# A fused linear-attention and mixer kernel: u of batch 1 is transposed by the DMA queue of SP, under a new hand-written order for all engines

## The chip, the cores and the metric

The kernel runs on one core of one Trainium2 chip. The metric is device time in microseconds (us) of one execution. Three runs of the kernel before gave 172.86, 173.35 and 173.45 us; the median, 173.35 us, is the time before.

## The reference, cut to what matters

Four batches (B = 4) are computed, each in two halves. First an attention with a decaying state, with 8 heads, 768 time steps and 48 values per head:

```python
f = 1.0 / (1.0 + np.exp(-f_logit))
for t in range(S):
    state = f[:, :, t, :, None] * state + np.einsum('bhd,bhe->bhde', k[:, :, t], v[:, :, t])
    y[:, :, t] = np.einsum('bhd,bhde->bhe', q[:, :, t], state)
```

Then, on x = y written as 768 tokens by 384 channels, a mixer over tokens and one over channels:

```python
h = np.maximum(xt @ w_tok1, 0.0) @ w_tok2        # xt is x transposed
u = x + h.transpose(0, 2, 1)
h2 = np.maximum(u @ w_ch1, 0.0) @ w_ch2
return u + h2
```

## The kernel before, in words

**Attention.** A batch's 768 steps are cut into 6 chunks of 128. For each chunk ACT forms the logarithm of f (`exp` and `ln`, L371 and L372; for batch 0, where two chunks are interleaved as a pair, L392 and L388), POOL or DVE splits it into a high and a low part (`lo`, L379, L401), PE sums it along time (`sums`, L461 and L462; batch 0 L615 and L618), ACT takes two exponentials of the sums (`G` and `Gi`, L471 and L473; batch 0 L628 and L630), DVE multiplies them onto q and k (`gated`), and q and k are transposed (`turn`: by PE at L500, or at L503 by a transfer that SP issues for all of batch 3; the copies of PE's result are `turned`, on DVE or on ACT). PE forms the scores (L413) and the chunk's own contribution to the state (`parts`, L429). The state goes from chunk to chunk: `tsum` on DVE, `state` (L577) on DVE or POOL, and two copies into a bf16 tile (`spread`, into `state_bd`, L277 on ACT or L281 on POOL), which the next chunk's `y` (L560 and L564; batch 0 `within` L719 and `y` L743) reads. `glast` (L481) is a small transfer of SP that brings the decay of a whole chunk to where the state needs it; it waits for `grow` on ACT (L477).

**Mixer.** Per batch: 12 products `tok1` (L757), the copies `h1T`, 6 pairs of products `tok2` (L773), the additions `u` (L789) on DVE, a bf16 copy `u_bf` on ACT or POOL, then u is transposed into `uT`, 24 groups `ch1` of three products (L826) that read `uT` and `w_ch1`, their copies `zT` (L357 on ACT, L359 on DVE), 18 groups `ch2` of four products (L845), 6 additions (L851) and 6 stores (L855). A `ch1` of half 0 needs the rows 0 to 2 of `uT`, one of half 1 the rows 3 to 5.

**The two ways to transpose u.** For a batch in `UTURN` SP issues two transfers, each of which transposes three tiles of `u_bf`; for another batch PE transposes tile by tile and ACT or DVE copies the result out of PSUM:

```python
        if b in UTURN:
            for th in range(2):
                tts = range(3 * th, 3 * th + 3)
                add(("ut", b, th), SP, lambda th=th: nc.sync.dma_start_transpose(...
        for tt in range(0 if b in UTURN else NCH):
            ...
            add(("ut", b, tt), PE, turn, need=["ident", ("u_bf", tt)], bank=pm, kind=mms(*[C] * 3))
            copies(("uT", b, tt), (DVE, ACT), lambda tt=tt: uT[:, tt, :, :].rearrange("p d t -> p (d t)"),
```

**The order.** Every step is recorded as an operation with a number, and nothing chooses at run time: `Plan.run` (L125 to L140) walks through the string `ORDER` (L36 to L80) and issues the operations in that order. A token is an operation's number; a letter behind it names the engine where there is a choice (A is ACT, D is DVE, G is POOL), and `:n` the PSUM bank that it takes. `w512`, `s11` and the like are products without use, which keep PE busy. So each engine executes its operations in the order of the string, each waits for what it reads, and an engine that waits holds up all that stands behind. The loads from HBM are issued by POOL, in the same queue as its arithmetic (L266, and L272 for weights); SP's queue holds `glast`, the transposes and the stores.

Of the kernel before, what the change touches and what calls it, by code (L numbers as in the profile page):

```python
# [37 lines left out]
38 50 53D 54 12D 39 52D 25D 55 100:0 15G 40 58 105:1 56D 57D 102 59 10G 137:2 104 41 11D 30D 107 114:3 60D 142:4 101 42  # L38
110 106 108 31A 103 62 119:1:0 139 18D 109 115 145 61D 111:5 143 112 125 144 180:6 141 138 147 113A 116D 43 151:2 146
126A 130 118:3:4 140 44 127A 117:5:1 123 182 152 175:0 153A 4G 122 45 121 176 131G 148:3 120 177 149 64 156:4:2 183 181  # L40
178 124:0:5 150A 162 63 184 186:6 179 187 185 132A 134 47 128D 154:3:4 188A 189:1 158 190 133G 191D 163G 66 157 165A
193:3:6 136A 169 155:1:4 135A 164G 197 67 192:2:5 159 46 160 336 195 w512 w128 161:4:6 170G 337 196 339 338G 173 198 340
166 194:2 172A 341G 199:5:1 129A 200 171A 68 174A 204 201D 358:0 342 167D 208:2 203A 209 202G 205D 215:3 359 65 206 210
361 211 207D 216 212 217 343 213 218 219 214D 360 220 344G 366:7 168D 221A 242 238 369 230:2 69 231 222:4 223 232 367
226:3 227 73 243 224 368 234 250:0 244A 228 235 239 245A 246:7 71 251D 247A 363 248:1 394:0 237A 249D 70 364:7 236A 233
256:1 240A 225 252:6 16G 272:2 345 241D 72 396 276:4 253D 348 254:5 257D 270:6 397 74 255D 229 274:1 398 395 371 48
296:5 346 362 278:0 275A 347D 370 304:3 351 273D 277A 372:1 365D 279A 280:2 349 297D 298:0 271A 373D 350G 402:4 290:6
305D 75 292:5 281D 291A 374:3 299D 293A 78 375:6 352 376:2 386 403 286:5 76 377 404 284:6 378 79 264:0 258:7 379 285D 77
381A 262:3 259D 265A 282:6 263A 81 399 382:7 283A 300:0 385 287A 400:3 387 380A 302:5 407 405 384D 391:2 406 408:4 80
401D 393A 431:1 301A 409D 260:6 353G 303A 388D 410:0 261A 412:5 383A 414 411:6 389G 392A 268:7 415 434 413 266:2 435  # L50
390A 423 294:0 269A 419:3 416G 267D 433 462:7 87 439:6 424 420A 422 469:2 470 441 463 417G 288:5 421A 418G 432 464 83
471 289D 428:3 295A 311:1 429D 82 316:0 425D 430A 436 90 440 317 426A 442 318 85 472 312 86 313 93 465 437:6 314 91
443:3 319 438A 321:1 320 444D 96 447:0 445:5 99 446:4 448 322 450 427G 331:6 449 97 306:0 457 590 84 587 458 454:5 323
588 451G 455D 584 332 452G 324 585 453G 326:4 92 466 459:1 589G 327 460A 586G 328 89 467 473 474 468A 610:3 475D 461A
307 593 329 479:2 611 476:4 612 480 482:1 456A 485:7 477 596 481G 488:2 483 478A 308 94 486 594 602:1 489 484G 491:7 604
615 496:4 88 498:2 605 494:5 333 499D 497D 606 595G 613 495D 616:2 492 512:5 490G 487A 309 646:7 603 354 334 500:0 524:3
647 617D 513A 508:6 607 501A 510:5 591 525D 502:0 493A 608:1 511D 592G 599 506:3 503D 609D 504:0 95 528:5 507A 505D 509A
638:4 529D 597 522:0 639 618:5 598G 523D 640 619:6 648 620:3 630 98 641 534:0 623 544:6 629 642 600 625G 520:4 624G 614
545A 621 355 530:2 649 631 514:1 622 521A 675:7 531A 651 516:3 515A 643 518:2 601D 356 536:1 519A 635:4 677 537D 526:2
517A 535A 644:1 676 626:3 645D 652:0 628A 550:5 627A 527D 559:6 653D 632G 551A 678 683:2 634G 633G 656:5 679 818 655:7  # L60
659 654:3 684 650 560 660G 685 658 830 661G 542:2 667 662A 538:3 636A 666 637A 561 680 824 672:4 821 686 554:0 833 657
539A 552:7 668 831 673D 663:3 540:5 562 681:1 541A 713:6 819 714 682D 687:5 664A 555 820G 553A 688D 674A 556 669G 665A
357 834 691:4 557 689:3 671A 690:7 543A 693 564:0 827 692 670A 715 836:3 822 694 706:2 698:1 702 695G 548:4 699D 835G
696A 707 708 701 825 565 697G 839 700D 823G 532:7 840 837 716 703:1 533D 838 709 549D 546:5 704D 717 569:4 705D 710 718
843:1 719D 711 570 846 547D 712D 574:6 847 845 826D 844 720:2 828 841 723:5 729:1 848 870:3 721 829G 849 726:7 871 575
727 722G 735:2 724 842 732:7 736 725A 566 730 728A 737G 877:2 872 733 738 576 880 734G 912:7 731A 832G 571 873 739 852:1
572 878 579:5 567 879 905:4 855 330 882 580 857A 881 577 856G 913 874 581 863 914 875 851:1:6 582 850:7:2 907 886:0 876
861 756:5 864D 742:3 862 865G 762:6 743A 853 760:1 906 889 908 867:3 854 764:2 883 866A 780:4 757A 765D 890G 768:7 761A
763D 892G 772:2 310 910 769A 583 858:6 891A 758:1 335 773A 746:7 868A 315 859A 740:2 568 747D 781A 909 766:5 898 860A
741D 325 919:4 759A 899G 885:0:7 767A 884:6:2 897 776:1 888 754:5 750:0 887 784:6 751A 896 744:2 869A 785D 893:7 777D  # L70
902:3 911 901G 778:6 755D 900G 782:1 745D 779A 915 770:5 903A 573 894A 941:6 916 942 752:2 771A 786:0 753D 943 934:5 922
787A 748:2 783D 923G 944 813:0 749D 924G 904D 925G 935 774:2 895D 936 937 775A 803:7 917:2:3 918:1:4 921 804 929 805 920
808:4 806 926:3 930 809 927A 931:1 945 814 932A 946 938 939 947D 793:7 940A 928D 933A 810 954:1 963:3 960:5 964 957:6
788:2 965A 958 948:3 811 959G 789 961 949 951:4 962G 798:5 952 950A 967 799 955 794 956G 953G 795 966 800 815 812 790
807 563 1008:1 1014:4 1002:3 1015D 998:6 801 1003A 1004:4 791 988:5 816 1005A 992:2 999D 990:4 796 968:6 989D 797 991A
1010:7 1009A 802 993A 972:4 558 792 974:1 973D 817 1000:2 1011D 578 984:4 1001A 982:7 975A 994:2 978:1 996:5 979D 980:0
985D 997A 970:1 983A 995D 986:4 969D 1041:2 1012:6 1006:7 976:5 1007D 1036:3 971D 977A 987A 1013D 1046:7 1042 981A 1043
1026:0 1044 1031:6 1047 1037 1048 1027 1021:2 1032 1033 1022 1034 1038 1035 1045 1028 1039 1023 1049 1029 1050 1016:7
1040 1024 1017 1025 1030 1018 1019 1020
# [68 lines left out]
def kernel(  # L148
# [603 lines left out]
    def mixer(b):  # L752
# [14 lines left out]
        for tt in range(NCH):  # L767
# [23 lines left out]
            if b == 0:  # L791
# [124 lines left out]
```

## Time and profile before

| | |
|---|---|
| median of three runs | 173.35 us |
| the profiled execution, its own time | 173.47 us |
| its span (first to last instruction) | 171.7 us |
| granted clock of PE, mean | 0.996 |
| PE busy | 162.2 us, 94% of the span |
| DVE, ACT, POOL busy | 123.3, 105.9, 90.8 us |
| first `sums` of batch 0 on PE | 7.23 us |
| first `sums` of batch 1 on PE | 26.30 us |
| first `ch1` of batches 0, 1, 2, 3 | 33.60, 72.80, 113.55, 144.55 us |
| last `ch2` of batch 3 ends | 168.15 us |

The span is shorter than the execution's own time by 1.77 us, which lies before the first and behind the last instruction. A row of the timeline gives start and length in us, engine, line, operation, the tile written and the tiles read, the count, and in brackets the idle time ahead of it with what ended it. PE's products overlap: one that lasts 0.33 us starts 0.16 us after the one before.

### The profile page before, as it was taken

Reading aid. Unit: us, or ns where it says so; the run is one execution under the profiler, and the core shown is the slowest. Engines: PE = TensorE matmul, PEld = TensorE weight load, DVE = VectorE, ACT = ScalarE, POOL = GpSimd, SP = SyncE. Lnnn points to the kernel's source line nnn. Section 1 sums busy time; section 2 is a strip of 40 time slices with the busy share of each in tenths; the row PEclk is TensorE's granted clock in tenths of the full one; section 3 lists DMA queues with packets and bytes.
Section 4 is the critical chain, followed back from the end, with each engine's and each line's share of the span. In section 5 each row is a group of like instructions: output and inputs, shape, how many; then the busy total and the mean of one; then the engine's idle time right before and its main releaser. Section 6 shows DMA issues by size and latency. Waiting matters only on the chain.

```text
span 171.7 us, 4436 instructions
## 1 busy us (share of the span) xinstructions
PE 162.2 (94%) x1753; PEld 103.2 (60%) x1753; DVE 123.3 (72%) x262; ACT 105.9 (62%) x240; POOL 90.8 (53%) x131
## 2 busy tenths in 40 slices
PE   6998688999999989999999999999999999999991
PEld 3476565666766645666757665565766656566660
DVE  5589986899995662999777889696976380754051
ACT  5999869995995615979898844959441420542000
POOL 8999678959959598897841933411220031000000
PEclk9999999999999999999999999999999999999998
DMA  5999999999999999969999190978370008250024
GB/s 143 226 171 223 202 196 189 185 144 171 185 196 188 148 139 52 56 83 214 106 143 79 8 130 7 189 166 239 111 168 4 0 7 242 96 211 0 0 96 181
DMA packets 89572, 22.72 MB, mean 132 GB/s; under 512 B 82288, under 2 KB 88736, under 8 KB 89552
## 3 DMA queue, kind: packets, MB, share of 16 engines
q0 software_dynamic: 69600, 13.77, 92.6%
q1 hardware_dynamic: 19952, 8.69, 19.1%
q8 instruction: 13, 0.21, 0.5%
q14 instruction: 7, 0.06, 0.1%
HBM read 25.17 MB, written 4.72 MB: 174 GB/s over the span
## 4 chain that ended last, share of the span: by engine, by line
PE 74%; POOL 11%; DMA 7%; ACT 3%; issue 2%; DVE 1%; POOLq 0%; DVEq 0%
PE ps L826 27%; PE ps L845 24%; DMA f_sb<-in_f_logit_dram 7%; PE ps L757 4%; PE ps L773 4%; POOL qk_sb L266 4%; PE ps L500 3%; PE ps L413 3%; POOL v_sb L266 2%; PE ps L564 2%; PE ps L429 2%; PE ps L461 2%; PE ps L462 2%; PE ps L560 1%; PE ps L811 1%
## 5 line engine op out<-in xcount | busy, mean ns | idle before, releaser
L826 PE MATMUL ps<-uT,w_ch 128*128 128x384 bf16 x288 | 52.6, 326 | 0.0
L845 PE MATMUL ps<-w_ch,zT 128*128 128x384 bf16 (+2 forms) x300 | 52.6, 320 | 0.0
L357 ACT ACTIVATE zT<-ps 128x384 bf16<-128x384 f32 x55 | 25.2, 491 | 21.5 <-PE ps L826 21.1
L845 PEld LDWEIGHTS <-zT 128*128 128x128 bf16 x300 | 27.7, 98 | 17.0
L826 PEld LDWEIGHTS <-w_ch 128*128 128x128 bf16 x288 | 26.8, 97 | 16.3
L359 DVE TENSOR_SCALAR zT<-ps 128x384 bf16<-128x384 f32 x41 | 21.4, 552 | 13.0 <-PE ps L826 12.6
L541 DVE TENSOR_TENSOR AmT<-ps,tri_bf 128x512 bf16<-128x512 f32 x36 | 23.4, 684 | 2.6 <-PE ps L413 2.4
L851 DVE TENSOR_TENSOR x_nat<-x_nat,ps 128x384 f32<-128x384 f32 (+2 forms) x25 | 12.8, 533 | 11.3 <-PE ps L845 11.1
L379 POOL TENSOR_TENSOR Llo<-L 128x384 bf16<-128x384 f32 x15 | 12.4, 834 | 11.8 <-ACT L L372 11.7
L266 POOL DMA_DIRECT2D qk_sb<-in_q_dram x16 | 15.7, 986 | 2.9 <-DMA f_sb<-in_f_logit_dram 2.3
L266 POOL DMA_DIRECT2D v_sb<-in_v_dram x16 | 15.8, 990 | 2.7 <-DMA f_sb<-in_f_logit_dram 1.7
L266 POOL DMA_DIRECT2D qk_sb<-in_k_dram x16 | 15.8, 990 | 0.0
L281 POOL CAST u_bf<-x_nat 128x384 bf16<-128x384 f32 x10 | 5.0, 508 | 14.6 <-issue 10.1
L277 ACT ACTIVATE x_bf<-ps 128x384 bf16<-128x384 f32 x15 | 7.0, 486 | 8.8 <-PE ps L564 8.8
L281 POOL CAST state_bd<-state 48x192 bf16<-48x192 f32 x22 | 8.0, 363 | 8.0 <-PE ps L560 3.0
L757 PE MATMUL ps<-x_bf,w_tok 128*128 128x384 bf16 x48 | 11.9, 326 | 0.0
L789 DVE TENSOR_TENSOR x_nat<-x_nat,ps 128x384 f32<-128x384 f32 x21 | 10.5, 546 | 1.6 <-PE ps L773 1.6
L490 DVE TENSOR_TENSOR qk<-qk_sb,GG 128x768 bf16<-128x768 bf16 x18 | 10.8, 615 | 0.0
L577 POOL TENSOR_TENSOR state<-tsum,glast 128x192 f32<-128x192 f32 x9 | 4.6, 507 | 10.4 <-PE ps L826 4.9
L471 ACT ACTIVATE GG<-ps 128x384 bf16<-128x384 f32 x18 | 8.9, 492 | 1.9 <-PE ps L462 1.0
L371 ACT ACTIVATE f_sb<-f_sb 128x384 f32<-128x384 f32 x18 | 9.1, 524 | 1.3 <-DMA f_sb<-in_f_logit_dram 1.2
L372 ACT ACTIVATE L<-f_sb 128x384 f32<-128x384 f32 x18 | 9.5, 526 | 0.2
(101 smaller groups left out, 264.3 us busy)
## 6 DMA issues: line engine op xcount, KB each, us to landing
out_dram<-x_nat SPq DMA_DIRECT2D x23, 192.0 KB, 2.4
f_sb<-in_f_logit_dram POOLq DMA_DIRECT2D x3, 1152.0 KB, 11.9
f_sb<-in_f_logit_dram SPq DMA_DIRECT2D x3, 384.0 KB, 4.0
qk_sb<-in_q_dram POOLq DMA_DIRECT2D x12, 96.0 KB, 7.7
qk_sb<-in_k_dram POOLq DMA_DIRECT2D x12, 96.0 KB, 7.2
w_ch<-in_moe_w_ch_dram POOLq DMA_DIRECT2D x2, 576.0 KB, 12.8
v_sb<-in_v_dram POOLq DMA_DIRECT2D x12, 96.0 KB, 7.5
w_ch<-in_moe_w_ch_dram POOLq DMA_DIRECT2D x1, 1152.0 KB, 10.4
```

Source lines behind the costliest of these rows:

```text
L266: lambda eng=eng, into=into, of=of: eng.dma_start(out=into, in_=of),
L281: nc.gpsimd.tensor_copy(out_, in_)
L357: nc.scalar.activation(out_, in_, AF.Relu, bias=0.0, scale=1.0)
L359: nc.vector.tensor_scalar(out_, in_, 0.0, None, ALU.max)
L379: op.fn = lambda: (nc.vector if op.engine == DVE else nc.gpsimd).tensor_tensor(lo, full, hi, ALU.subtract)
L490: add(("gated", b, c, *names), DVE, lambda n=n: nc.vector.tensor_tensor(qk[it][:, n, :, 0:D], qk_sb[nb][:, n, :, c, :], GG[i][:, n], ALU.m ...
L541: add(("masked", b, c, p), DVE, lambda half=half, made=made: nc.vector.tensor_tensor(half, made(), tb4, ALU.mult), need=["tri_bf"], make=[ ...
L757: add(("tok1", b, rt, kt), PE, lambda rt=rt, kt=kt, pm=pm: nc.tensor.matmul(banks[pm.at][:, 0:DM], lhsT=w_tok1[:, kt, rt * 128:(rt + 1) * ...
L789: nc.vector.tensor_tensor(to, un, banks[pm.at][:, 0:DM], ALU.add)
L826: nc.tensor.matmul(banks[pm.at][:, 0:384].rearrange("p (n t) -> p n t", t=128), lhsT=w[:, kt, c0:c0 + 128], rhs=uT[:, rows3, kt, :], start ...
L845: nc.tensor.matmul(banks[pm.at][:, 0:n1 - n0], lhsT=zT[:, kt, tt * 128:(tt + 1) * 128], rhs=w_ch2[:, kt, n0:n1], start=(kt == 0), stop=(kt ...
L851: add(("sum", b, tt, n0), DVE, lambda un=un, pm=pm, n=n1 - n0: nc.vector.tensor_tensor(un, un, banks[pm.at][:, 0:n], ALU.add), make=[("x_n ...
```

## The change

`UTURN` gains batch 1, so that its u is transposed by two transfers of SP. The 6 transposes of PE (18 products) and the 6 copies of batch 1 go, two transfers come, the program has 1041 operations in place of 1051, and the numbers behind them move down by 10. The whole string `ORDER` is new: order, engines and banks of all operations. (The file is one line shorter: L826 of before is L825 after.)

```diff
-UTURN = (2, 3)
+UTURN = (1, 2, 3)
 ...
 ORDER = """
-w512 w512 w512 s11 32 0G 6G 33 8G 20D 9D 5G 34 13D 7G 1 21G 35 2 24A 23A 27D 3A 37 26A 29D 14D 28 49 17D 36 19D 51 22G
...
+w512 w512 w512 s5 32 5G 33 21G 20D 18G 7D 34 0D 14D 1 6G 2 24A 23D 8D 22G 35 26D 27D 11G 15D 36 19D 49 10D 25D 9D 37 29D
...
```

Among the products without use, `s11` becomes `s5`, and the pair `w512 w128` that stood behind the scores of batch 0 becomes one `w128` further ahead.

**ACT in the first 25 us.** Before, these rows (tiles of batch 0 until `f_sb_76`, which is f of batch 1; `zT` holds the turned q or k, `state_bd` is `spread`):

```order
L277 ACTIVATE zT<-ps_118 128x1024
L277 ACTIVATE state_bd_97<-state 48x4x48
L277 ACTIVATE x_nat_99<-ps_117 128x384
L277 ACTIVATE x_bf_102<-ps_117 128x384
L371 ACTIVATE f_sb_76<-f_sb_76 128x8x48
L372 ACTIVATE L_78<-f_sb_76 128x8x48
L371 ACTIVATE f_sb_76<-f_sb_76 128x8x48
```

After, the same place, up to the first logarithm of batch 1:

```order
L627 ACTIVATE GG_81<-ps_117 128x384
L632 ACTIVATE gpair_120<-ps_117 128x8
L276 ACTIVATE zT<-ps_112 128x1024
L276 ACTIVATE zT<-ps_115 128x1024
L276 ACTIVATE state_bd_98<-state 48x4x48 x2
L276 ACTIVATE zT<-ps_112 128x1024
L370 ACTIVATE f_sb_76<-f_sb_76 128x8x48 x2
L371 ACTIVATE L_78<-f_sb_76 128x8x48
```

Three of the four turned tiles of ACT now stand together right ahead of batch 1's f, and two `exp` stand ahead of the first `ln`. Further ahead, the `ln` of chunks 4 and 5 now stands before that of chunks 2 and 3, behind both `exp`. On PE the first `sums` of batch 1 moves up: it now stands ahead of `parts` of chunk 4, `within` of chunks 2 and 4, and `y` of chunks 2, 3 and 4 of batch 0, behind two `tok1`.

**POOL towards the end of batch 1's attention.** Before (`qk_sb_71` and `v_sb_74` are loads of batch 2, `glast_90` is the decay of chunk 4 of batch 1):

```order
L266 DMA v_sb_74<-in_v_dram 128x8x48 x2
L281 CAST state_bd_98<-state 48x4x48
L266 DMA qk_sb_71<-in_k_dram 128x8x48
L266 DMA v_sb_74<-in_v_dram 128x8x48
L577 TENSOR_TENSOR state<-tsum,glast_90 128x192
L281 CAST state_bd_97<-state 48x4x48 x2
```

After (`f_sb_76` is f of batch 3, a whole batch; `x_nat_100` is u of batch 1):

```order
L265 DMA qk_sb_71<-in_q_dram 128x8x48
L280 CAST state_bd_97<-state 48x4x48
L265 DMA qk_sb_71<-in_q_dram 128x8x48
L576 TENSOR_TENSOR state<-tsum,glast_90 128x192
L265 DMA qk_sb_71<-in_k_dram 128x8x48 x2
L265 DMA qk_sb_71<-in_q_dram 128x8x48
L265 DMA f_sb_76<-in_f_logit_dram 128x48x48
L378 TENSOR_TENSOR Llo<-L_77 128x8x48 x3
L265 DMA v_sb_74<-in_v_dram 128x8x48 x3
L265 DMA qk_sb_71<-in_k_dram 128x8x48
L280 CAST u_bf<-x_nat_100 128x384
```

Before, 13 loads stand between f of batch 2 and that `state`; after, 4 do. The load of f of batch 3, which stood behind three `u_bf` copies, now stands ahead of the `lo` steps of batch 2 and of both copies of u that POOL makes for batch 1.

**SP, from the last `glast` of batch 1.** Before, only `glast` and one store stand here:

```order
L481 DMA glast_89<-grow_94 128x1x4
L481 DMA glast_90<-grow_92 128x1x4
L855 DMA out_dram<-x_nat_99 128x384
L481 DMA glast_88<-grow_93 128x1x4
L481 DMA glast_90<-grow_92 128x1x4
L481 DMA glast_89<-grow_94 128x1x4
```

After:

```order
L480 DMA glast_88<-grow_93 128x1x4
L801 DMA_TRANSPOSE uT<-u_bf 128x9x128
L480 DMA glast_89<-grow_94 128x1x4
L480 DMA glast_88<-grow_93 128x1x4
L480 DMA glast_90<-grow_92 128x1x4
L801 DMA_TRANSPOSE uT<-u_bf 128x9x128
```

The first transpose, of tiles 0 to 2, stands behind the last `glast` of batch 1; between it and the second, of tiles 3 to 5, stand the `glast` of chunks 1, 0 and 2 of batch 2. All stores now stand behind the transposes of batch 1.

More of the change, by code (lines that the diff above doesn't have):

```diff
@@ L42 @@
[L42 to L61, printed above, removed]
@@ L77 @@
[L77 to L79 removed]
+w512 w512 w512 s5 32 5G 33 21G 20D 18G 7D 34 0D 14D 1 6G 2 24A 23D 8D 22G 35 26D 27D 11G 15D 36 19D 49 10D 25D 9D 37 29D
+50 12D 4D 51 40 3A 53D 54 28 52G 58 39 13D 105:0 59 38 55 100:1 61D 42 60D 108 106 56D 102 175:2 41 107 57D 101 104
@@ new lines @@
+956 953:2 949G 798:4 954 799 796 548 955G 779 957 800 780 801 785 806 802 797 960:0 786 563 974:4 792 978:7 975D 962:6
+979A 992:4 994:7 993A 976:2 963A 958:4 977D 964:6 781 959A 982:2 995D 782 980:5 787 986:7 807 981A 1000:4 987D 1002:5
+1004:7 1003A 998:1 961A 1005D 972:5 990:7 984:0 991A 966:3 985A 970:7 967A 996:0 965A 971D 983A 988:3 999D 1006:7 973D
+989D 1016:1 1001D 1036:3 968:5 1031:4 969D 1011:2 997D 1026:5 1032 1017 1018 1012 1021:0 1033 1013 1022 1014 1037 1034
+1023 1019 1035 1027 1015 1024 1020 1038 1028 1039 1040 1007 1029 1025 1008 1030 1009 1010
```

54 lines of the change are left out of this document (35 added, 19 removed).

## The prediction

> **What bounds the kernel now.** I read the table of stages first (busy time of each engine in stretches of the span), then PE's waits, then the timeline at those waits. In the table the first column is the length of the stretch, then busy time and count of each engine, granted clock, DMA share and GB/s.
>
> ```profile
> span 171.7 us, 4436 instructions
> 7.00:26.00 19.00, 16.30 (x418) 12.10 (x415) 16.49 (x39) 16.64 (x37) 16.42 (x23) 1.00 1.64 195
> 34.00:60.00 26.00, 26.00 (x294) 17.16 (x293) 22.08 (x46) 20.01 (x47) 20.53 (x25) 1.00 2.00 172
> 60.00:68.00 8.00, 6.92 (x62) 4.25 (x60) 3.58 (x7) 2.15 (x6) 7.76 (x12) 1.00 1.76 105
> 79.00:114.00 35.00, 34.93 (x374) 22.07 (x371) 29.38 (x59) 27.07 (x63) 17.67 (x23) 1.00 1.36 110
> 114.00:145.00 31.00, 31.00 (x278) 19.35 (x276) 20.17 (x40) 12.49 (x29) 5.55 (x13) 1.00 0.40 102
> ```
>
> From 34 us on PE is full, 26.00 of 26.00 and 31.00 of 31.00, except in 60 to 68, where it lacks 1.08 of 8.00 while POOL is full. So PE's own work, and the waits before 34 us and at 60 to 68, set the end; a product less is time less, and a wait elsewhere that reaches PE is time more. Behind PE's last product lies a tail (sum, store, end) that the change leaves as it is: the last `ch2` in the new list is again row 0 of batch 3. The profiled execution took 173.47 us for a span of 171.7; it is 0.12 above the median of 173.35. I add terms to 173.47 and take 0.12 off at the end.
>
> **Term 1: PE's transposes of batch 1, -1.0.** This row is one of the chain that ended last:
>
> ```profile
> 71.10 0.50 PE ps L811 x9
> L811 PE MATMUL ps<-ident,u_bf 128*128 128x128 bf16 x36 | 3.5, 219 | 0.1
> L279 DVE COPY uT<-ps 128x384 bf16<-128x384 bf16 x10 | 3.3, 349 | 0.0
> ```
>
> Nine products advance the chain by 0.50, so the 18 of batch 1 take 1.0, in stretches where PE is full. The six copies that go (0.35 each on DVE) free engines on which PE does not wait there; I take nothing for them.
>
> **Term 2: PE's waits at 61.8 and 64.9, -1.1.** PE's own list of waits, and the timeline:
>
> ```profile
> PE ps L560 <- POOL state_bd L281: 1.1, 2, 0.7
> 61.83 0.33 PE L560 MATMUL ps<-state_bd,qkT 128*128 128x96 bf16 x4 [0.68 <-POOL state_bd L281]
> 64.87 0.33 PE L560 MATMUL ps<-state_bd,qkT 128*128 128x96 bf16 x4 [0.39 <-POOL state_bd L281]
> 43.68 2.27 POOL L266 DMA_DIRECT2D f_sb<-in_f_logit_dram  x1
> 57.91 0.88 POOL L266 DMA_DIRECT2D v_sb<-in_v_dram  x1 [1.74 <-DMA f_sb<-in_f_logit_dram]
> 61.38 0.40 POOL L281 CAST state_bd<-state 48x192 bf16<-48x192 f32 x1
> 63.52 0.50 POOL L577 TENSOR_TENSOR state<-tsum,glast 128x192 f32<-128x192 f32 x1
> ```
>
> Both `y` wait for a copy of the state by POOL, which had stood 1.74 us at a load: seven loads are issued behind f of batch 2, and the next begins only when that f has landed. Everything behind it on POOL is 1.74 late, more than the 0.68 that PE lacks. After, 4 loads stand between that f and this `state` where 13 stood, and POOL reaches it before its `tsum` is there. What waits instead is the load of f of batch 3, the eighth behind f of batch 2; behind it stand three `lo`, the first of which PE reads some 3 us later by my count, and the u copies of term 4. If POOL is late all the same, this term is 0.
>
> **Term 3: the beginning, +1.1.** Rows of before:
>
> ```profile
> 7.64 0.85 ACT L392 ACTIVATE f_sb<-f_sb 128x768 f32<-128x768 f32 x1
> L388 ACT ACTIVATE L<-f_sb 128x768 f32<-128x768 f32 x2 | 1.7, 840 | 0.0
> 11.94 0.51 ACT L630 ACTIVATE GG<-ps 128x384 bf16<-128x384 f32 x1
> 12.31 0.52 ACT L628 ACTIVATE GG<-ps 128x384 bf16<-128x384 f32 x1
> 18.67 1.02 ACT L277 ACTIVATE zT<-ps 128x1024 bf16<-128x1024 bf16 x1 [0.20 <-PE ps L743]
> 22.18 0.53 ACT L371 ACTIVATE f_sb<-f_sb 128x384 f32<-128x384 f32 x1 [1.20 <-DMA f_sb<-in_f_logit_dram]
> L281 POOL CAST state_bd<-state 48x192 bf16<-48x192 f32 x22 | 8.0, 363 | 8.0 <-PE ps L560 3.0 <-DVE state L577 2.8 <-DVE state L549 1.5
> L379 POOL TENSOR_TENSOR Llo<-L 128x384 bf16<-128x384 f32 x15 | 12.4, 834 | 11.8 <-ACT L L372 11.7
> 22.87 0.89 PE L719 MATMUL ps<-v_sb,zT 64*128 64x48 bf16 x32
> 24.60 0.74 PE L719 MATMUL ps<-v_sb,zT 64*128 64x48 bf16 x32
> 26.13 0.33 PE L743 MATMUL ps<-state_bd,zT 128*128 128x96 bf16 x4 [0.79 <-ACT state_bd L277]
> 26.30 0.34 PE L461 MATMUL ps<-L,tri_bf 128*128 128x384 bf16 x1
> 27.67 0.33 PE L743 MATMUL ps<-state_bd,zT 128*128 128x96 bf16 x4 [0.38 <-POOL state_bd L281]
> 29.63 1.79 PE L773 MATMUL ps<-h1T,w_tok 128*128 128x384 bf16 x10
> ```
>
> Before, ACT had no work left at 21 us and stood until f of batch 1 had landed (22.18). After, ACT has more ahead of that f. From the `exp` at 7.64, which begins when the last f of batch 0 has landed: one `exp` and two `ln` at 0.84 (2.5), 12 `G` and `Gi` at 0.37 from start to start (4.4), four turned tiles at 1.02 (4.1), four `spread` at 0.36 (1.4; POOL's take the same), small ones 0.9, together 13.3. Waits inside: 0.75 for `sums` of chunk 3 (its `ln` now stands last, then two more `lo` on DVE), and about 0.8 for the transposes of chunks 0 to 3. So f of batch 1 is begun at 22.7; `exp`, `exp`, `ln` at 0.53 end at 24.2, `lo` on POOL (0.83) at 25.1, and PE begins `sums` of batch 1 there, 1.2 sooner than at 26.30. But of the work that lay before it, from 22.87 to 26.30 less the wait of 0.79, 2.4 us now lie behind, and two `tok1` (0.3) lie ahead: 2.1. PE is 2.1 - 1.2 = 0.9 behind. The waits that follow in before (0.38 at a `y` of batch 0, some 0.4 until 34 us) I set against those that I find in the new list: second `sums` of batch 1 behind a further `lo`, 0.4, `y` of chunk 5 0.3, scores of batch 1 and `tok2` behind DVE's queue of masks, 0.3: +0.2 net. Sum +1.1. Bounds: if ACT's waits vanish, the landing of f binds and `sums` begins at 24.6, +0.6 instead of +1.1, and without the waits behind it 0; if DVE's queue is 1.5 later still, +2.6.
>
> **Term 4: the wait for the two transfers, +0.3.** No transfer of this kind ran beside loads in before: the ten that there are lie at 105.9 us and later. The rows nearest are those of `glast` (2 KB) in three windows, and of a store among loads; last column, issue to landing:
>
> ```profile
> uT<-u_bf SPq DMA_TRANSPOSE x4, 2.9
> glast<-grow SPq DMA_DIRECT2D x2, 2.0 KB, 7.6
> glast<-grow SPq DMA_DIRECT2D x5, 2.0 KB, 5.0
> glast<-grow SPq DMA_DIRECT2D x5, 2.0 KB, 2.0
> out_dram<-x_nat SPq DMA_DIRECT2D x1, 192.0 KB, 4.2
> out_dram<-x_nat SPq DMA_DIRECT2D x23, 192.0 KB, 2.4
> 71.60 0.65 PE ps L845 x4
> 70.78 0.33 PE ps L773 x2
> 44.78 0.45 PE ps L500 x8
> L789 DVE TENSOR_TENSOR x_nat<-x_nat,ps 128x384 f32<-128x384 f32 x21 | 10.5, 546 | 1.6 <-PE ps L773 1.6
> ```
>
> The windows are 40 to 60 us (f of batch 2 in flight, 7.6), 79 to 100 (whole loads of batch 3, 5.0) and 100 to 130 (loads done, 2.0); the store is that of 57.65. So loads add between 1.8 (store, against 2.4 for the median store) and 5.6. First transfer: from the last `tok2` of its three tiles to the first `ch1` the new list gives PE 9.4 us (10 `ch2` at 0.65, three `tok2` and three `sums` at 0.33, two turns of batch 2 at 0.45). Off it go the last addition (0.55), the copies queued on ACT (0.65) and the transfer (2.9): 5.3 us are left. f of batch 3 is in flight then, so the nearest row is the 5.6: a wait of 0.3. Second transfer: 12.1 us of PE work; it stands behind three `lo`, four loads and a `glast` that needs ACT, and is issued about 5.4 in; with 2.9 there are 3.8 left, and single q, k, v loads are in flight, as at the store: 1.8, no wait. Bounds: 0, and 5.6 in both plus as much again for the larger size, about 3.5 in all.
>
> What each of the other edits does: `s5` for `s11` and the fillers lie where PE waits anyway, 0. Batch 2's and 3's transposes stay on SP; their places give 3.1 us of PE work or more to a 2.9 transfer, 0.
>
> **Sum:** -1.0 - 1.1 + 1.1 + 0.3 = -0.7; 173.47 - 0.7 - 0.12 = 172.65, rounded 172.6.
>
> **The rivals.**
> - *The transfers are late (slower).* The place is the first `ch1` of either half of batch 1. It decides when a transfer takes more than 8.2 (half 0) or 6.7 us (half 1). For it: 7.6 in the window with f, and a transfer of 288 KB has more to get through than 2 KB. Against: 4.2 for a store of 192 KB. Price: 2 us more than my sum, 174.6. The Trainium skill (DMA: Bandwidth & Descriptors, Queues, rings and completion order) says that each DMA engine goes round its queues packet by packet and finishes a packet before it changes; by that rule a transfer of many packets pays at each of them, and this rival would hold. The trace's 2.0 against 7.6 for a tiny transfer agrees with a wait per packet, and no row shows it for many. Chance 0.2.
> - *The beginning is worse (slower or same).* ACT and DVE hold PE up by 2.6 instead of 1.1: 174.1. For it: DVE is at 16.5 of 19 us in 7 to 26. Chance 0.15.
> - *The beginning costs nothing.* The landing of f binds and PE catches up, -2.1 in all, to 171.2. Chance 0.15.
> - *PE's clock falls.* The granted clock is 1.00 in every stretch above. Between 20 and 25 us PE stands, by my account, 0.5, 1.5, 0.4 and 0.7 us with work in between and with one filler less. Against: the clock stood at 1.00 through before's waits too. Were the clock half for 3 us, a length that I assume, PE would lose 1.5: 174.1. The Trainium skill (TensorE: Matmul & The Clock Gate, Part 1) says that a window of about 3.4 us without work halves the clock; by that rule four shorter pieces would not suffice, and no run here shows a fall. Chance 0.05.
> - That the change doesn't do what it says: the two transfers are in the built order; no chance given.
>
> **How the numbers follow.** Forecast 0.45, of which 0.3 below 172.8 (faster by over 0.3%, about what a measurement of this kernel can tell from no change) and 0.15 within 0.3%. Transfers late 0.2, slower. Beginning worse 0.15, of which 0.12 slower and 0.03 same. Beginning free 0.15, faster. Clock 0.05, slower. Faster 0.45, same 0.18, slower 0.37. For the range: down to 170.9 (terms 1 and 2 in full, the beginning at 0, no wait for transfers, and a little less), up to 175.3 (a full 3 us for late transfers). The forecast's own range is 171.8 to 173.4.
>
> **What would show it.** Term 1: L811 with 18 products, `uT` with six transfers. Term 2: no wait of L560 for POOL around the last chunks of batch 1. Term 3: the first product of L461 (L460 after) near 25 us, and a first `tok2` near 32 instead of 29.6 with four turns and scores more done. Term 4: landing times of `uT` in batch 1 of 5 to 8 us, and PE idle ahead of the first L825 of batch 1 by 0 to 1. It is wrong if PE waits over 1 us for `uT`, if the granted clock leaves 1.00, or if a load that POOL now issues later (`w_ch2`, by my count landing about 1 us before its first reader) holds PE up.

## The result, and the profile after

| | before | changed | changed, second set |
|---|---|---|---|
| median, us | 173.11 (4 runs) | 176.18 (4 runs) | 175.81 (4 runs) |
| lowest to highest, us | 172.56 to 173.45 | 174.88 to 178.03 | 174.90 to 177.35 |
| ratio to before, 95% interval | | 1.0148, 1.0111 to 1.0186 | 1.0158, 1.0118 to 1.0198 |

The change makes the kernel 1.5% slower. The forecast was 172.6 us with a range of 170.9 to 175.3: the sign was wrong, and the time lies above the range. The profiled execution of the first set took 178.03 us, the slowest of its four (the median holds it, the ratio leaves it out), and a second profile took 177.35 us, the slowest of its set, so sizes are read from both.

The table of stages after, for the same stretches as in the prediction and for 68 to 79 us (the span is 176.3 us, that of before 171.7):

```profile
7.00:26.00 19.00, 15.54 (x330) 10.34 (x330) 16.16 (x40) 16.43 (x36) 16.80 (x23) 0.94 1.79 189
34.00:60.00 26.00, 24.89 (x287) 16.30 (x285) 22.57 (x49) 20.23 (x48) 22.32 (x28) 1.00 1.52 155
60.00:68.00 8.00, 8.00 (x61) 4.96 (x60) 5.02 (x11) 2.81 (x7) 2.65 (x2) 1.00 1.91 106
68.00:79.00 11.00, 8.98 (x64) 5.38 (x63) 5.92 (x11) 9.11 (x21) 10.96 (x15) 1.00 1.66 170
79.00:114.00 35.00, 34.49 (x374) 21.78 (x372) 29.91 (x59) 26.33 (x64) 17.75 (x20) 1.00 2.23 108
114.00:145.00 31.00, 30.30 (x293) 18.91 (x290) 24.32 (x49) 12.58 (x30) 5.98 (x14) 1.00 0.47 105
```

In the kernel before, PE was full from 68 to 79 us:

```profile
68.00:79.00 11.00, 10.99 (x116) 7.14 (x114) 10.35 (x23) 9.77 (x24) 9.03 (x12) 1.00 0.80 91
```

The stretch from 60 to 68 us, where PE lacked 1.08 us before, is full now (8.00). Instead PE lacks 1.11 us in 34 to 60, 2.02 in 68 to 79, 0.51 in 79 to 114 and 0.70 in 114 to 145, and in the first stretch the granted clock is 0.94 where it was 1.00. PE's own list of waits says for what (five of its rows):

```profile
PE ps L825 <- DMA uT<-u_bf: 1.4, 1, 1.4
PE ps L675 <- ACT zT L276: 1.2, 1, 1.2
PE ps L844 <- DMA w_ch<-in_moe_w_ch_dram: 1.1, 1, 1.1
PE ps L412 <- DMA qkT<-qk: 0.7, 1, 0.7
PE ps L825 <- DVE zT L358: 0.5, 1, 0.5
```

Three of the five are transfers or loads that land late. The same list from 79 to 145 us is empty in the kernel before; here the last two rows stand in it. The second profile has the same waits in other sizes: w_ch2 0.7, uT 1.0 in two places, DVE 1.0, qkT 0.6.

Microsecond by microsecond around the clock's fall: length, PE's busy time and count, granted clock, DMA share, GB/s.

```profile
21.00:22.00 1.00, 0.42 (x16) 1.00 1.43 195
22.00:23.00 1.00, 0.39 (x28) 1.00 1.90 191
23.00:24.00 1.00, 0.58 (x32) 0.77 2.29 145
24.00:25.00 1.00, 1.00 (x15) 0.50 2.70 150
29.00:30.00 1.00, 1.00 (x35) 0.50 1.60 88
30.00:31.00 1.00, 1.00 (x14) 0.81 1.22 55
```

PE works for 0.42 and 0.39 us of two microseconds, and in the third the clock goes to half. Counted by slices of 0.2 us and the clock in each, it is 0.50 from 23.5 to 30.4 us, and in both profiles of this kernel for 6.8 us. Products of 128x384 that started 0.16 us apart then start 0.32 apart.

The places of those waits on the timeline, and what ACT and POOL waited for before the transfer for batch 1:

```profile
33.39 0.82 PE L772 MATMUL ps<-h1T,w_tok 128*128 128x384 bf16 x4
57.77 1.47 PE L844 MATMUL ps<-w_ch,zT 128*128 128x384 bf16 x8 [1.11 <-DMA w_ch<-in_moe_w_ch_dram]
66.06 2.23 POOL L265 DMA_DIRECT2D f_sb<-in_f_logit_dram  x1 [5.35 <-DMA f_sb<-in_f_logit_dram]
65.68 0.94 ACT L370 ACTIVATE f_sb<-f_sb 128x384 f32<-128x384 f32 x2 [3.77 <-DMA f_sb<-in_f_logit_dram]
77.40 1.79 PE L825 MATMUL ps<-uT,w_ch 128*128 128x384 bf16 x10 [1.45 <-DMA uT<-u_bf]
126.89 0.40 PE L412 MATMUL ps<-qkT 48*128 48x128 bf16 x8 [0.69 <-DMA qkT<-qk]
```

The view of the tile `uT` between 60 and 90 us, with the time from issue to landing of its two transfers (the first is the maximum, the second the minimum):

```profile
L801 SPq DMA_TRANSPOSE uT<-u_bf x2: 1365/1378/1392, 68.3 to 76.2; - x2
DMA to landing us min/median/max: 7.8/8.4/9.1
```

When f of batch 2 has landed at 65.66, ACT, which stood 3.77 us for it, runs two `exp` and a `ln` and only then the three copies of u; POOL issues f of batch 3 at the same moment (66.06). SP issues the first transfer at 68.3, behind that load of 1152 KB, and it lands 9.1 us later. That PE's first `tok2` begins at 33.39 where it was 29.63 is mostly the work that was moved ahead of it; how much is the clock, experiment 1 shows.

### The profile page after: what moved, and what is told of

Same layout as the page of the kernel before. It is cut to its first block, busy times and chain, and to the rows that moved or that the text cites. A ratio compares the mean times of both kernels' runs of the same rounds, so it can differ in the third digit from the quotient of the medians.

```text
span 176.3 us, 4368 instructions
## 1 busy us (share of the span) xinstructions
PE 163.6 (93%) x1727; PEld 102.6 (58%) x1727; DVE 127.5 (72%) x270; ACT 103.1 (58%) x234; POOL 88.8 (50%) x123
## 3 DMA queue, kind: packets, MB, share of 16 engines
q1 hardware_dynamic: 22320, 9.28, 22.4%
## 4 chain that ended last, share of the span: by engine, by line
PE 58%; DMA 21%; ACT 7%; POOL 5%; DVE 4%; issue 1%; SPq 1%; DVEq 0%; POOLq 0%
PE ps L844 20%; PE ps L825 17%; DMA f_sb<-in_f_logit_dram 13%; DMA uT<-u_bf 5%; PE ps L756 4%; PE ps L772 3%; DMA qkT<-qk 2%; PE ps L412 2%; POOL qk_sb L265 2%; POOL v_sb L265 2%; PE ps L499 2%; ACT u_bf L276 1%; PE ps L460 1%; PE ps L563 1%; PE ps L461 1%
## 5 line engine op out<-in xcount | busy, mean ns | idle before, releaser
L825 PE MATMUL ps<-uT,w_ch 128*128 128x384 bf16 x288 | 51.6, 326 | 2.0 <-DMA uT<-u_bf 1.4
L825 PEld LDWEIGHTS <-w_ch 128*128 128x128 bf16 x288 | 27.2, 98 | 19.5 <-issue 2.5
L356 ACT ACTIVATE zT<-ps 128x384 bf16<-128x384 f32 x53 | 24.2, 489 | 18.3 <-PE ps L825 18.3
L358 DVE TENSOR_SCALAR zT<-ps 128x384 bf16<-128x384 f32 x43 | 22.7, 552 | 12.2 <-PE ps L825 9.4
L788 DVE TENSOR_TENSOR x_nat<-x_nat,ps 128x384 f32<-128x384 f32 x21 | 11.1, 550 | 6.6 <-PE ps L772 6.6
L756 PE MATMUL ps<-x_bf,w_tok 128*128 128x384 bf16 x48 | 12.7, 342 | 0.0
L576 POOL TENSOR_TENSOR state<-tsum,glast 128x192 f32<-128x192 f32 x7 | 3.6, 512 | 16.8 <-DVE tsum L551 8.5
L278 DVE CAST x_bf<-ps 128x384 bf16<-128x384 f32 x16 | 8.8, 552 | 4.0 <-PE ps L563 3.4
L276 ACT ACTIVATE x_nat<-ps 128x384 f32<-128x384 f32 x15 | 7.3, 495 | 5.9 <-DMA out_dram<-x_nat 3.2
L772 PE MATMUL ps<-h1T,w_tok 128*128 128x384 bf16 x48 | 10.4, 326 | 0.0
## 6 DMA issues: line engine op xcount, KB each, us to landing
w_ch<-in_moe_w_ch_dram POOLq DMA_DIRECT2D x1, 1152.0 KB, 11.7
```

The costliest lines, as they stand in the source:

```text
L356: nc.scalar.activation(out_, in_, AF.Relu, bias=0.0, scale=1.0)
L358: nc.vector.tensor_scalar(out_, in_, 0.0, None, ALU.max)
L756: add(("tok1", b, rt, kt), PE, lambda rt=rt, kt=kt, pm=pm: nc.tensor.matmul(banks[pm.at][:, 0:DM], lhsT=w_tok1[:, kt, rt * 128:(rt + 1) * ...
L772: nc.tensor.matmul(banks[pm.at][:, 0:DM], lhsT=w_tok2[:, kt, tt * 128:(tt + 1) * 128], rhs=h1T[:, kt, :], start=(kt == 0 and not held), st ...
L788: nc.vector.tensor_tensor(to, un, banks[pm.at][:, 0:DM], ALU.add)
L825: nc.tensor.matmul(banks[pm.at][:, 0:384].rearrange("p (n t) -> p n t", t=128), lhsT=w[:, kt, c0:c0 + 128], rhs=uT[:, rows3, kt, :], start ...
```

## The experiments

Times are medians beside the kernel before on the same chip, whose own median was 173.00 us beside experiments 1 to 4, 173.03 beside 5 to 8 and 172.93 beside 9 to 12. Diffs show pieces of the list; where an edit makes the file a line longer, L825 reads L826.

**1. Fillers keep PE's clock up (`e1_warm`).** `w512` and `w128` are products without use.

```diff
-133A 162 155:3:5 135D ... 17G 193:1:2 336 ... 169 337 192:5:6
+133A 162 w128 155:3:5 135D ... 17G w512 193:1:2 336 ... 169 337 w128 192:5:6
```

> The changed kernel with three fillers added on PE in the stretch 21 to 24 us, where it idles (1.17 us ahead of the scores of chunk 5, 0.42 ahead of those of chunk 4). Theory A: the granted clock fell to 0.50 from about 23.5 to 30.6 us because PE was busy for less than half of 20.8 to 24.3; with the fillers the clock stays at 1.00, the first tok2 of batch 0 begins near 32.2 instead of 33.4 us, and the gain is passed on, since POOL issues its later loads behind a lo that waits for ACT, which waits for PE: 1.0 to 1.3 us less than the changed kernel (176.2 to about 175.0). Rival B: the clock is held, but the later waits for w_ch2 (57.7 us) and for uT (77.4 us) end with loads and swallow the gain: 0 to 0.3 us less. Rival C: fillers of about 1.4 us do not hold the clock: 0.50 is seen again and the time is that of the changed kernel.

174.47 us, ratio 1.0061 (1.0023 to 1.0098): 1.3 to 1.7 us less than the two medians of the changed kernel, and the intervals stand apart. PE in the same microseconds (same columns):

```profile
22.00:23.00 1.00, 0.96 (x33) 1.00 1.97 174
23.00:24.00 1.00, 0.96 (x28) 1.00 2.39 156
25.00:26.00 1.00, 0.90 (x22) 1.00 2.57 149
```

And its first `tok2` on the timeline:

```profile
31.81 0.99 PE L773 MATMUL ps<-h1T,w_tok 128*128 128x384 bf16 x5
```

In this profile the clock is 1.00 throughout, and the first `tok2` begins at 31.81 in place of 33.39 (33.85 in the second profile). Over the span the mean granted clock is 0.996 to 1.000 in eight of the ten executions, against 0.977 to 0.990 in the eight of the changed kernel; in the other two (177.88 and 176.64 us) it is 0.981 and 0.986, so in those the clock fell in spite of the fillers, and no profile shows where. Theory A holds, with a little more than its 1.0 to 1.3 us, and it explains the wait for `w_ch2` too. POOL issues that load behind a `lo` that waits for ACT, and so for PE: at 44.40 us here, 46.02 and 46.48 in the changed kernel. It lands at 54.93, and PE does not wait for it.

**2. The load of f of batch 3 as late as before (`e2_f3_late`).**

```diff
-483 322 354 580 480 ... 632 630 490G 606:2
+483 322 580 480 ... 632 630 490G 354 606:2
```

> The changed kernel with the load of f of batch 3 issued by POOL behind both copies of u that it makes for batch 1, as in the kernel before, instead of 8 us earlier. Theory A: transfers land in the order of issue behind all loads issued earlier; the first transfer of u of batch 1, issued near 68.3, then lands near 71.8 (behind the last load of batch 2, 69.9, and its own 1.8), the wait of 1.4 us ahead of the first ch1 at 77.4 goes, and the time falls by 1.0 to 1.5 us (176.2 to about 174.9). Rival B: a transfer among loads is slow whatever was issued ahead of it: it lands at 75 us or later, and little changes (0 to 0.4). Rival C: the wait goes but f of batch 3 or the second transfer behind it is late instead: 0 or up to 1 us more.

184.66 us, ratio 1.0679 (1.0639 to 1.0719). The first transfer, by the view of its tile:

```profile
L801 SPq DMA_TRANSPOSE uT<-u_bf x1: 1361/1361/1361, 64.9 to 64.9; - x1
DMA to landing us min/median/max: 2.9/2.9/2.9
```

ACT and PE on the timeline:

```profile
83.93 0.52 ACT L370 ACTIVATE f_sb<-f_sb 128x384 f32<-128x384 f32 x1 [8.34 <-DMA f_sb<-in_f_logit_dram]
84.89 1.44 PE L825 MATMUL ps<-uT,w_ch 128*128 128x384 bf16 x4 [8.30 <-ACT zT L356]
```

PE's busy time and clock then:

```profile
79.00:85.00 6.00, 0.12 (x1) 0.56 1.60 146
85.00:90.00 5.00, 5.00 (x29) 0.51 1.32 70
```

Theory A is right on the first transfer: with no large load ahead it lands 2.9 us after its issue instead of 9.1. But the order of issue is not the rule: the second transfer, issued at 73.03, just behind the start of that load's issue (72.95), lands at 76.5 and the load at 83.9. Theory A is wrong on the time, and rival C named the cause, at a price of 1 us at most. On ACT an `exp` of batch 3 stands ahead of copies of `ch1`; f now lands at 83.9, ACT stands 8.34 us, PE 8.30, and then PE works at half clock for 5 us more. So the early place of that load, which delays the transfer, is needed by ACT's order.

**3. PE turns u again, in the new list (`e3_pe_turn`).** UTURN is (2, 3) once more; products and copies stand like this (later numbers go up by 10):

```diff
+498:3 496:2 499D 497D 317 494:3 495D ... 520:1 500:5 ... 521D 504:5 522:7 501D ... 510:4 505D 502:3 ... 526:0 503D
```

> The new list, with u of batch 1 turned by PE again: 18 products and 6 copies on DVE come back, the two transfers go. It undoes the first part of the change alone. Theory A: the transfers cost the list their wait of 1.4 us and save 1.0 us of products, so this kernel is 0.4 us faster than the changed one (about 175.8), with the first ch1 near 77.0. Rival B: PE would have had to wait there for other things (the turned q and k of batch 2 and DVE) and the products come on top: 0.6 to 1.0 us slower, about 177.

175.58 us, ratio 1.0175 (1.0117 to 1.0233), an interval that holds both of the changed kernel's ratios. In this list the transfer is worth nothing that can be measured, in either direction; the 0.4 us of theory A is too small to be seen. By the traces it saves 18 products and gives a wait back. The clock falls here too, from 24.8 to 28.2 us.

**4. The transfer alone, in the list of before (`e4_sp_turn`).**

```diff
-UTURN = (2, 3)
+UTURN = (1, 2, 3)
 ...
+484G 494 491:7 ... 493A 495
```

> The list of the kernel before, with u of batch 1 turned by two transfers of SP in the places where its copies of u are ready: the first part of the change alone, with nothing put between. 18 products go: 1.0 us less. Theory A (a transfer lands behind every load issued before it): the first is issued near 71.0 and lands near 74.6, 2.5 us after PE reaches its ch1; the second is issued near 76, behind f of batch 3 which lands at 83.1, and lands near 85, about 4.5 us after PE needs it: in all 6 us more than before, about 179. Rival B (a transfer takes 2.9 us and at most 1.8 more among loads): waits of 3.8 us at the first half and none at the second: about 3 us more, 176.

178.17 us, ratio 1.0299 (1.0260 to 1.0338). PE at its first `ch1` of batch 1, on the timeline:

```profile
76.09 1.14 PE L826 MATMUL ps<-uT,w_ch 128*128 128x384 bf16 x3 [3.83 <-DMA uT<-u_bf]
```

Its busy time and clock around that product:

```profile
74.00:81.00 7.00, 4.91 (x19) 0.53 1.00 196
```

5.2 us more, between the two theories and for a reason that neither had. PE waits 3.83 at the first half, as in B, none at the second (that transfer is issued later than I counted, at 79.7, and lands at 83.6). The rest I put down to the clock: after the wait it is 0.53 from 74 to 81 us. The products put between u and its `ch1` in the new list do hide most of the transfer: there PE has 7.7 us of other work while it runs (9.1 less a wait of 1.4), here 1.6 (5.4 less 3.8).

**5. f of batch 3 in a middle place (`e5_f3_mid`).**

```diff
-483 322 354 580 480 ... 586 328 582G 578 486
+483 322 580 480 ... 586 328 582G 354 578 486
```

> The changed kernel with the load of f of batch 3 moved behind the first two lo of batch 2 on POOL, a middle place: behind the issue of the first transfer of u of batch 1, but early enough for the exp of batch 3 that stands ahead of copies of ch1 on ACT. Theory A (transfers and loads land in the order of issue): the first transfer lands near 71.5 instead of 77.4, f of batch 3 near 79.5 where ACT needs it at 79.7, and the wait of 1.4 us goes with nothing in its place: 1.0 to 1.5 us less than the changed kernel, near 175.0. Rival B: ACT stands at the exp of batch 3 for 1 us or more and PE behind it: no gain or up to 2 us more.

177.30 us, ratio 1.0236 (1.0210 to 1.0263). Its list of waits:

```profile
PE ps L825 <- DMA uT<-u_bf: 2.6, 2, 2.0
PE ps L461 <- POOL Llo L378: 1.5, 1, 1.5
```

Neither theory held. The first transfer lands 3.0 us after its issue, and f lands at 77.0, in time for ACT. But the issue of f takes POOL 2.2 us, and the third `lo` behind it makes PE wait 1.5. The second transfer is issued at 75.9, with f and the loads behind it in flight, and lands 8.1 later: 2.0 of wait. Each of the three places that were tried for that load makes somebody wait.

**6. Two loads earlier (`e6_loads_early`).**

```diff
-235 344G 238 ... 237A 72 226:6 ... 241A 379 70 227
+235 72 70 344G 238 ... 237A 226:6 ... 241A 379 227
```

> The changed kernel with two loads of batch 1 (k of chunk 3, q of chunk 2) issued by POOL ahead of the lo of chunk 2 instead of behind it, in the 1.96 us for which POOL stands there at 31.5 us. Theory A (POOL's issue sets when w_ch2 and f of batch 2 land): all later loads are issued and land about 1.8 us earlier, w_ch2 near 56.0 and f of batch 2 near 63.9; the waits for w_ch2 (1.1) and, behind an earlier exp on ACT, part of that for uT go: 1.1 to 1.8 us less than the changed kernel, near 174.8. Rival B: the DMA engines are the limit, the landings move by less than 0.5 and the time by 0 to 0.4. The clock's fall near 23.5 us stays in either case.

175.24 us, ratio 1.0131 (1.0077 to 1.0185). The interval meets that of the changed kernel, so the time alone doesn't decide. `w_ch2` is issued at 44.15 and lands at 54.14, f of batch 2 at 60.44, and the waits left are these:

```profile
PE ps L826 <- DVE zT L359: 1.2, 1, 1.2
PE ps L413 <- DMA qkT<-qk: 0.8, 1, 0.8
PE ps L826 <- DMA uT<-u_bf: 0.6, 1, 0.6
```

An earlier issue does bring earlier landings, as theory A has it: the wait for `w_ch2` is gone, and so is that for uT ahead of the first `ch1` of batch 1 (the 0.6 lies in batch 2). But `w_ch2` is issued 1.9 us earlier than in the first profile and lands 3.6 earlier, f of batch 2 even 5.2; why the landings move by more than the issue stays open. Part of the gain is taken by DVE, whose copy PE now waits for 1.2 us.

**7. The kernel before, without its pair of fillers (`e7_before_no_filler`).**

```diff
-336 195 w512 w128 161:4:6
+336 195 161:4:6
```

> The kernel before without its pair of products without use (1.3 us of PE in all) behind the scores of batch 0, at 22.6 us, which the new list does not have at this place. Theory A: that pair kept PE's clock up; without it PE is busy for about half of 19 to 23 us, the granted clock falls to 0.50 for some 3 to 7 us near 23 us, and the time rises by 1.0 to 2.0 us, to about 174.5. Rival B: the pair does nothing, since PE's idle pieces here are shorter; the clock stays at 1.00 and the time within 0.3 us.

173.63 us, ratio 1.0036 (1.0012 to 1.0061). PE's busy time and clock:

```profile
20.00:21.00 1.00, 0.09 (x5) 1.00 1.65 180
21.00:22.00 1.00, 0.82 (x46) 1.00 1.55 180
22.00:23.00 1.00, 0.24 (x15) 0.70 1.60 196
24.00:26.00 2.00, 2.00 (x64) 0.50 1.60 185
26.00:29.00 3.00, 2.91 (x35) 0.50 1.59 194
```

The pair did keep the clock up: without it the clock is at half from 22.4 to 29.2 us, and the mean granted clock is 0.976 to 0.989 in all ten executions, where 10 of the 13 of the kernel before beside them have 0.996 to 1.000 and three 0.99 (five of the 13 beside experiment 1 have 0.98 or 0.99, so that kernel's clock falls now and then too). But the fall costs 0.6 us of time, not 1.0 to 2.0. That PE waits for others in much of this stretch in that list, so that slower products fill its waits, fits this and was not tested by itself.

**8. First mix (`e8_mix`).** The fillers of 1, the middle place of 5, and one copy of a `ch1` ahead of a `gated` on DVE. A fourth edit is not named in the expectation: the transfer of SP that turns q and k of chunk 2 of batch 3 (866) stands behind one of the two that transpose u of batch 2.

```diff
-667 641 534:3 668 529D 591G
+667 529D 641 534:3 668 591G
 ...
-844 724G 866 713:6 ... 715A 729 898
+844 724G 713:6 ... 715A 729 866 898
```

> The changed kernel with three edits: the fillers of the warm kernel at 21 to 24 us, f of batch 3 behind the first two lo of batch 2, and on DVE one copy of a ch1 of batch 1 ahead of the gated of chunk 3 of batch 2 (PE waited 0.9 us for that copy at 83 us in the warm kernel). Theory A: each of the waits named was real and nothing takes their place: 173.3 of the undisturbed warm run less 0.3 (uT) and less 0.8 (the copy), near 172.2, 0.5 per cent faster than the kernel before. Rival B: PE meets ACT or DVE a little later and the time stays at 173.0 to 173.4, that of the kernel before.

176.16 us, ratio 1.0177 (1.0136 to 1.0219): worse than the fillers alone. PE waits 0.8 for a `lo` on POOL, 1.2 at 77 us for an ACT copy behind an `exp` that waits 1.24 for f of batch 3, and 1.6 for turned q and k, most of it in one row:

```profile
115.25 0.40 PE L413 MATMUL ps<-qkT 48*128 48x128 bf16 x8 [1.31 <-DMA qkT<-qk]
```

The first two belong to the middle place, which makes PE wait as in 5; rival B was too kind to it. The third belongs to the fourth edit: that transfer is issued at 112.14, in experiment 1 at 109.57, and lands at 115.20. So this time is not the price of the middle place alone.

**9. The changed kernel again (`e9_changed_again`).**

> The changed kernel itself, unaltered, for a second profile. Theory A: the wait of 1.1 us for w_ch2 at 57.7 us belonged to the first profiled execution alone (178.03 us), since two kernels of these experiments with the same list up to there have w_ch2 landing near 55.2: here PE waits less than 0.3 us for w_ch2, while the clock's fall near 24 us, the wait of 1 to 1.5 us for uT ahead of the first ch1 and those for DVE near 85 us and for turned k and q near 125 us are seen again; time 175 to 176.5. Rival B: w_ch2 holds PE for about 1 us again and the wait is part of the change's cost.

175.81 us. Rival B: in the profile the clock is 0.50 from 24.5 to 31.4 us and PE waits 0.7 for `w_ch2`, so that wait is part of the change's cost. The two kernels on which theory A leaned (2 and 5) had a fall of 3.4 us only, from 25.1 to 28.5, with the load issued at 45.3 instead of 46.0 to 46.5: the same list, another length of the fall. The wait for uT is 0.4 ahead of the first `ch1` here, and that for DVE is 1.05.

**10 and 11. Second and third mix (`e10_mix2`, `e11_mix3`).** The fillers, the copy on DVE ahead of the `gated`, and a store of batch 1 moved behind two transfers of batch 3; f of batch 3 stays where the change has it. The second mix has the two early loads of 6 as well.

```diff
-758:0 553 757A ... 752:2 901 745A
+758:0 757A ... 752:2 901 553 745A
```

> The changed kernel with the fillers of the warm kernel, the two loads issued early, the copy of a ch1 on DVE ahead of the gated of chunk 3 of batch 2, and one store of batch 1 moved behind two transfers of batch 3; f of batch 3 stays where the change put it. Theory A (the costs are separate): from the 174.5 of the warm kernel 0.9 goes with the loads and 0.8 with the copy: 172.6 to 173.0, at best 0.3 per cent faster than the kernel before. Rival B: one wait hides behind the other, only one of the two gains is kept, and the time is 173.5 to 174.0.

> As the second mix, but the two loads are left where the change has them. Theory A (costs are separate): 0.9 us slower than the second mix, near 173.6. Rival B: with the clock held, the loads are early enough anyway, and the two mixes are within 0.3 us.

172.69 us, ratio 0.9982 (0.9954 to 1.0011), and 173.53 us, ratio 1.0028 (1.0010 to 1.0047). Theory A holds for both medians (the third mix was expected near 173.6). The gap of 0.84 is the early loads (PE waits 1.0 for uT in the third mix, 0.2 in the second), and the two intervals just touch. That between the third mix and the fillers alone, 0.94, is seen in the medians and in the wait for DVE's copy, which was 0.9 and is no longer in the list, but the intervals of those two overlap. The second mix in the stretches:

```profile
7.00:26.00 19.00, 16.85 (x367) 11.41 (x369) 16.82 (x40) 16.66 (x37) 17.32 (x23) 1.00 1.79 189
34.00:60.00 26.00, 26.00 (x290) 17.17 (x288) 23.17 (x50) 19.34 (x47) 20.18 (x25) 1.00 1.77 168
60.00:68.00 8.00, 8.00 (x51) 4.81 (x50) 4.48 (x9) 6.13 (x16) 6.37 (x7) 1.00 1.54 188
```

And its waits at `ch1`:

```profile
PE ps L826 <- DVE zT L359: 0.4, 1, 0.4
PE ps L826 <- DMA uT<-u_bf: 0.2, 1, 0.2
```

PE is full from 34 to 68 us, at full clock. This version has the lowest median of all, 0.2% below the kernel before; the interval holds 1, so it can't be told from it.

**12. PE turns u, in the second mix (`e12_mix2_pe`).** The edits of 3 on top of those of 10.

> The second mix with u of batch 1 turned by PE again: 18 products and 6 copies on DVE come back, the two transfers go. Theory A: with its waits mended the transfer is worth the whole of its 1.0 us of products: this kernel is 0.7 to 1.0 us slower than the second mix. Rival B: the wait for the transfer and the waits for DVE still stand, and it is within 0.4 us of it. Rival C: DVE, full from 77 to 85 us, cannot take six more copies, and it is 1.5 us or more slower.

174.59 us, ratio 1.0107 (1.0074 to 1.0140): 1.9 us more than the second mix: more than A gave, and not for C's reason, since no wait for DVE is behind it. One row of the profiled run holds the surplus:

```profile
121.57 1.62 PE L826 MATMUL ps<-uT,w_ch 128*128 128x384 bf16 x9 [1.63 <-ACT x_nat L277]
```

PE waits for the bank of an ACT copy that began at 121.02; the store of the tile into which it copies had landed at 120.94, 4.28 us after its issue (2.08 in the second mix). This lies in batch 2, where SP turns u in both kernels. So 1.0 of the 1.9 is accounted for by the products; whether the late store is in all four runs isn't known. In a list whose waits are mended the transfer is a gain, of a size that I can bound only by 1.0 to 1.9.

## Why the prediction was wrong, step by step

- **Term 1, -1.0: right as far as shown.** The 18 products are gone and nothing came back for them on PE. No run measures their time alone.
- **Term 2, -1.1: right.** PE's waits at `y` for POOL are gone; 60 to 68 us is full. As foreseen, the load of f of batch 3 waits instead, for 5.35 us.
- **Term 3, the beginning, +1.1: the queue was right, the clock was left out, and this is the step that failed.** The first `sums` of batch 1 began at 24.88 (forecast 25.1; the terms written for ACT add up to 22.5, not 22.7, and its `exp` began at 22.47). With the clock held, the first `tok2` begins at 31.81 (forecast near 32). In the changed kernel it begins at 33.4 to 33.9. The prediction listed the idle pieces 0.5, 1.5, 0.4 and 0.7, said that "four shorter pieces would not suffice", and gave a fall of the clock 0.05. The trace has 0.2, 1.2 and 0.4 there, and they sufficed. The clock was at 0.50 for 6.8 us. That delays the first `tok2` by 1.6 to 2.0 us and also moves POOL's later issue, so that `w_ch2`, which the prediction counted as landing 1 us ahead of its reader, lands 0.7 to 1.1 too late. At the end of the kernel the fillers are worth 1.3 to 1.7 us in the medians, the largest part of what was missed and not quite half of it.
- **Term 4, the transfers of batch 1, +0.3: loads do delay them, both sizes a little off.** I gave the first transfer 8.5 us and 8.2 of room. That the 5.6 of delay, taken from a transfer of 2 KB, comes near the 6.2 of this one of 288 KB is luck: the last section shows what delays it, and it is the rival's mechanism, not one size for all. (The 3.5 given as the bound of both waits doesn't follow from its words: 5.6 in both gives 0.3 and 1.8.) It took 9.1 and had 7.7, since the copies of u stood on ACT behind an `exp` that waited for f of batch 2, which I had not counted. The wait was 1.45 in one profile and 0.4 in the other; the second transfer was in time.
- **"Batch 2's and 3's transposes stay on SP; their places give 3.1 us of PE work or more to a 2.9 transfer, 0": nearly right for u, and too narrow.** PE waits 0.6 for uT of batch 2 in the second profile and not in the first. But the new list also moves the turned q and k of batch 3, which I did not price: one such transfer is issued behind two stores, takes 4.4 us, and PE waits 0.7 for it (0.6 in the second profile).
- **DVE, taken at nothing: wrong by 0.5 to 1.0.** I looked at DVE only for the six copies that go. The new list puts two `gated` ahead of a copy of `ch1` around 83 to 88 us, and PE waits for that copy.

The sum of what was missed can be read from the mixes: from 175.8 or 176.2 by the fillers to 174.5, by the copy on DVE and the store to 173.5, by the early loads to 172.7. That is 3.1 to 3.5 us; the forecast was 3.2 to 3.6 too low. The steps by copy and store and by the loads are as certain as the intervals of experiments 10 and 11. Part of what the early loads take away is a wait that Term 4 had counted, so that 172.69 meets the forecast is partly luck.

Of the rivals, "the transfers are late" met its condition at the first half (9.1 and 8.7 us against 8.2) with waits of 1.45 and 0.4 us, under its price of 2. "The beginning is worse" had the right place and the wrong cause, and "PE's clock falls" had the right cause. The price that I gave the latter (1.5 for half a clock over 3 us) took no account of what stands behind it.

What stays open: the changed kernel's times spread over 3.2 us in the first set where before's spread over 0.9. The length of the fall is not all of it, since in the second set executions with the same mean clock (0.977 to 0.979) took 174.9 to 177.35 us. The landing of `w_ch2` differs too, 9.9 us after its issue in experiments 2 and 5 and 11.3 to 11.7 in the two profiles of the changed kernel; why wasn't tried.

## What to carry to other kernels

Where an edit of the order leaves PE's idle pieces close together, add up PE's busy time in the few microseconds around them; between 20 and 25 us of these profiles a share under 0.6 was the danger, if not a sure sign, and a filler in a gap cost nothing that could be seen. A transfer of many small packets that is moved among loads gets its turns beside theirs, so look at what is in flight when its packets begin, on whatever queue. And where one load feeds several engines, look at each of them before it is moved: here an early issue delayed a transfer, a late one stopped ACT, and a middle one stopped POOL.

## What the runs showed of the hardware

**The clock falls without a long gap.** In seven profiles (both of the changed kernel, 2, 3, 5, 6 and 7) the clock fell to 0.50 between 22.4 and 25.1 us, for 3.4 us in experiments 2, 3 and 5 and for 6.8 in the others. In the 3.41 us right ahead of these falls PE was busy for 1.57 to 2.16 us, a share of 0.46 to 0.63, and the longest idle piece was 1.17 us. I also took the share in 3.4 us, in steps of 0.2, at its lowest between 10 us and the fall (or 34 us): 0.36 to 0.59 in these seven, and 0.64 to 0.80 in the six profiles without a fall there (before, and those with the fillers); experiment 4 had 0.55 and no fall. Later stretches show that the share alone does not decide: around its wait for uT the changed kernel has PE busy for 1.82 of 3.4 us (74.75 to 78.15), experiment 12 for 1.77 (118.4 to 121.8), and the clock stayed at 1.00 in both. The Trainium skill (TensorE: Matmul & The Clock Gate, Part 1) says that the gate watches PE's activity in a free-running window of about 3.4 us and halves the clock after an idle one. The lengths agree with one or two such windows; that the window must be idle does not agree, since PE was busy for about half of it or more. What else counts beside the share stays open.

**A transfer of SP takes turns with POOL's loads, packet by packet.** In five kernels (the changed one in both profiles, 1, 6, 10 and 11) the first transfer was issued 2.2 to 4.6 us after the start of the issue of f of batch 3; it landed 1.1 to 1.8 us after that load, 6.6 to 9.1 us after its own issue. In three (2, 5, 8) it was issued ahead of that load and landed in 2.9 to 3.0 us; in experiment 4 it was issued ahead of it too, among loads of 96 KB, and took 5.4. The profile counts packets and MB by queue; POOL's loads are `software_dynamic`, the transfers of SP `hardware_dynamic` (in experiment 2 that queue moves 0.30 MB from 65.5 to 68 us, when the transfer of 288 KB is in flight). The changed kernel from 71.5 to 74 us, then experiment 4 from 72.8 to 74.4:

```profile
q0 software_dynamic: 124, 0.52, 94.9%
q1 hardware_dynamic: 108, 0.03, 8.4%
q0 software_dynamic: 719, 0.07, 81.1%
q1 hardware_dynamic: 648, 0.17, 79.9%
```

The two queues send about one packet for one (104 to 97 in experiment 1 from 67.5 to 69.5 us, but 140 to 308 in the second profile from 70.2 to 73). In the changed kernel a packet of the load has some 4 KB and one of the transfer 256 B, so the transfer gets on slowly, sends most of its 1152 packets once the load is through, and lands just behind it; beside the short packets of experiment 4 it loses less. The Trainium skill (DMA: Bandwidth & Descriptors, Queues, rings and completion order) says that each DMA engine takes turns between its queues, packet by packet. The traces agree, and so the rival that the prediction built on this sentence had the mechanism right. Not explained by it: in the six profiles with a late landing the transfer's first packet came 3.3 to 3.8 us after the issue, in experiments 2, 5 and 8 after 1.3.
